# Attention and gated FFN on one core: the product with V behind the first score tile, a couple's own mark, and query couples at half rate

## The chip, the core and the metric

The kernel runs on one core of a Trainium2 chip. TensorE (PE) multiplies, VectorE (DVE) and ScalarE (ACT) read its results from PSUM banks, GpSimd (POOL) does elementwise work on SBUF, SyncE (SP) issues DMAs. The metric is the device time of one execution in microseconds; lower is better. Before the change it is 1832.74 us, the median of three runs (1832.44 to 1833.5).

## The reference

A block of a transformer with adaptive layer norm: one sequence of 2048 rows of 512, attention with 32 query heads of 16 and a single key and value head, then a gated FFN with 1792 hidden columns.

```python
mod = (_silu(c) @ w_mod).reshape(c.shape[0], 6, 1, -1)
h = _layernorm(x, axis=-1) * (1 + ca) + sa
# attention: q = h wq (32 heads of 16), k = h wk, v = h wv (one head)
scores = jnp.einsum("bhqd,bkd->bhqk", q, k) * (Dh ** -0.5)
p = _softmax(scores, axis=-1)
o = jnp.einsum("bhqk,bkd->bhqd", p, v)
x = x + ga * (o @ wo)
h = _layernorm(x, axis=-1) * (1 + cb) + sb
x = x + gb * ((_sigmoid(h @ w_gate) * (h @ w_up)) @ w_down)
```

## The kernel before, in words

**Units and half-steps.** The attention is cut into 32 units: eight blocks of 256 query rows by four groups of eight heads. A unit runs over 16 key blocks of 128 rows; one key block of one unit is a *step*, 512 in all, and a step has two *half-steps* h = 0 and 1, 1024 in all. TensorE is split for this: a matmul takes 64 rows (one *row half*) and 32 columns, so that `columns` issues four matmuls that fill one row half, and the two halves can work at once.

**What a half-step issues.** The tuple `ORDER` (line 57) gives the order:

- `a0`, `a1`: two tiles of scores for the row maxima (tile name `sa`, 128 queries by 512 keys). DVE reduces each to its maximum (`mx<-sa`). They run ahead of the rest by 84 tiles (`A0`) and so end 42 half-steps before the loop does. Three banks.
- `s0`, `s1`: two tiles of transposed scores (`st`, 128 keys by 512 query columns). ACT writes the exponential of each to `P`. Two banks, so that a half-step's `s0` needs the bank that the half-step before filled with its own `s0`.
- `c`: the product of P and V, in float32 (`craw<-P,V`), for the step two earlier (`LAG`). It adds to one bank over the whole unit. A float32 matmul runs as two passes, so the trace has eight of them.

The score tiles use row half 1 - h and the product row half h; with every half-step they change places.

**Marks.** Two row halves must not add to one bank at the same time. So after a product `hand_over` issues a matmul with one column of zeros (`craw<-nought`) whose end raises the semaphore `turn`, and `take_over` waits until `turn` has reached the latest count, `done[0]`. The product waits so before it starts. What stands behind such a wait in the program waits too, since the instructions of an engine are issued in their order.

**Couples.** At the end of a half-step stands a *piece* of other work (`piece`, `plan`). Two groups of matmuls with a bank each, for queries (`pq`), the output product (`po`), gate and up (`pgu`) or down (`pd`), make a `Couple`: 24 *blocks* or more (a block is four matmuls on each row half). In its first leg, blocks 0 to m - 1, group 0 has row half 0 and group 1 row half 1; in the second they change halves. After the first leg a mark is handed over, before the second there is a `take_over`. A new couple uses the two banks that ACT and DVE have to empty of the last one.

**The planner.** `plan` spreads a couple's blocks over half-steps: `RATE` 2.2 a half-step, at most `MOST` 3, for FFN work; for query couples before step `FIRST` `QRATE` 0.9, at most one. Ten of the sixteen query groups are left for the loop, so there are five query couples. The FFN of a pair of units' rows (512 rows) joins once they are done; the first at step 137, the last pair's after the loop, in the tail, where matmuls are 128 x 128 and row halves are not used. What of the planned couples finds no room in the loop goes there too. Weights are loaded and split into two float16 parts on the way, one job every so many steps (`WSTEPS`); the last four, which overwrite the query weights, wait for step `WLAST`.

Of the kernel before, what the change touches and what calls it, by code (L numbers as in the profile page):

```python
# [53 lines left out]
HLO = ('PDPD', 'PPPP', 'PPPP', 'PPPP')  # L54

A0 = 84
ORDER = "a0", "c", "s0", "a1", "s1"
LAG = 2


# [3 lines left out]
GAP = 2  # L64
KEPT = 2
RATE = 2.2
QRATE = 0.9
MOST = 3
SWAP = 5
WSTEPS = 110  # L70
WLAST = 112
WLATE = 2
WSTORE = 5
FIRST = 75
QLEAD = 6
W1 = 2
W2 = 3
# [9 lines left out]
def adaln_mqa_glu_kernel(  # L87
# [48 lines left out]
    pe, dve, act = Ordered(nc.tensor), Ordered(nc.vector), Ordered(nc.scalar)  # L136
# [5 lines left out]
    def columns(dst, l_, r_, start, stop):  # L142
        for c_ in range(0, P, 32):
            pe.matmul(dst[c_:c_ + 32], l_[:, c_:c_ + 32], r_, start=start, stop=stop)

    turn, done, side, open_ = nc.alloc_semaphore("turn"), [0], [0], [False]
# [4 lines left out]
    def behind(later, earlier):  # L151
        tc.add_manual_dep(later.ins, earlier.ins.name,
                          mybir.DependencyInfo(mybir.DependencyClass.Sync, mybir.DependencyReason.DATA),
                          reason="a bank that Tile doesn't follow")

    def hand_over():
        g, rs = 32 * (done[0] // 2 % 4), slice(64 * side[0], 64 * side[0] + 64)
        z = pe.matmul(raw_c["c"][g:g + 32, 0:1], nought[rs], nought[rs, 0:1], start=False, stop=False)
        if not done[0]:
            behind(z, nought_set)  # L160
        done[0] += 1
        z.then_inc(turn, 1)
        tc.add_to_no_dep_group("turn", z.ins)
        tc.no_tile_sem_insts.add(z.ins.name)

    def take_over():
        pe.wait_ge(turn, done[0])

    class Group:
        def __init__(self, stage, n, name, term, end, begin=None, w=1):  # L170
# [17 lines left out]
    class Couple:  # L188
# [3 lines left out]
        def part(self, n0, n1):  # L192
            if n0 == 0:
                for g in self.gs:
                    g.open()
            m = self.gs[0].n
            for n in range(n0, n1):
                if n == m:
                    take_over()
                for j in range(2):  # L200
                    g = self.gs[j ^ (n >= m)]
                    l_, r_, *cut = g.term(n % m, slice(64 * j, 64 * j + 64))
                    columns(cut[0](g.bank) if cut else g.bank, l_, r_, n == 0, n == 2 * m - 1)
                if n == m - 1 and open_[0]:
                    hand_over()
            if n1 == self.n:
                for k, g in enumerate(self.gs):
                    g.end(g.bank, k == 1)
# [5 lines left out]
    def t32(name, shape=(P, 512)):  # L214
        return wp.tile(list(shape), F32, tag="f32", name=name, bufs=18)
# [284 lines left out]
    def q_group(b, o):  # L500
# [5 lines left out]
        def end(pq, second):  # L506
            qdone.add((b, o))
            q2 = wp.tile([P, 2, 512], F16, tag="q2", name="q2", bufs=2)
            q32 = t32("q32")
            if second and now[0] < FIRST:  # L510
                defer(1, lambda: q_evict(b, o, q2, q32, pq))
# [10 lines left out]
    def q_evict(b, o, q2, q32, pq):  # L522
        act.activation(q32, pq, AF.Identity, scale=1.0 / (SH * SW))
        pool.tensor_scalar(q2[:, 0], q32, 1.0, 0.0, op0=ALU.mult, op1=ALU.add)
        q_low(b, o, q2, q32)
# [110 lines left out]
    def pv(i, t, j):  # L636
        c_ = raw_c["c"]
        side[0] = j
        rs = slice(64 * j, 64 * j + 64)
        if (t, j) != (0, 0):  # L640
            take_over()
        for hh in range(4):
            z = pe.matmul(c_[32 * hh:32 * hh + 32, :], V[rs, t, :], Ps[i, t, hh][rs, :],
                          start=(t == 0 and j == 0), stop=(t == NKB - 1 and j == 1))
            if (t, j, hh) == (0, 0, 0) and i > 0:
                behind(z, raw_c["out"])
        open_[0] = (t, j) != (NKB - 1, 1)
        if open_[0]:
            hand_over()
        raw_c["last"] = z  # L650
        if j == 1:
            for hh in range(4):
                del Ps[i, t, hh]
            if t == NKB - 1:
                unit_end(i)
# [82 lines left out]
    def defer(n, f_):  # L738
        waits.append((now[0] + n, f_))
# [34 lines left out]
    class Transposes:  # L774
        stage, n = "tr", 4

        def __init__(self, part):
            self.part = part
# [214 lines left out]
    def places(m, hb, rate, most, skip, part):  # L993
        ws = []
        rate, most = rate / part, most / part
        while sum(ws) * rate < m + lead[0] / part - rate / 2 or sum(ws) * most < m:
            ws.append(0.0 if len(ws) < (skip or 0) else weight(hb + len(ws), skip is not None))
        lead[0] += part * (m - rate * sum(ws))
        ends = [round(m * sum(ws[:k + 1]) / sum(ws)) for k in range(len(ws))]
        return [k - z for z, k in zip([0] + ends, ends)]  # L1000
# [23 lines left out]
    def plan(s, hb):  # L1024
# [8 lines left out]
        else:  # L1033
            q = g.stage == "q" and s < FIRST
            rate, most = (QRATE, 1) if q else (RATE, MOST)
            sizes = []
# [22 lines left out]
    for i, (b, o) in enumerate(units):  # L1059
# [10 lines left out]
        for kb in range(NKB):  # L1070
# [12 lines left out]
            for h in range(2):  # L1083
                for z in ORDER:
                    k = int(z[1:] or 0)
# [15 lines left out]
            while wdone < nw:  # L1101
                if wdone < nw - 4 and (wdone + 0.5) * WSTEPS > (s + 1) * (nw - 4):
                    break
                if wdone >= nw - 4 and s < WLAST + 3 * (wdone - nw + 4):
                    break
# [66 lines left out]
```

## Time and profile before

| what | us |
|---|---|
| median of three runs | 1832.74 |
| the profiled execution | 1831.11 |
| its span, first to last instruction | 1829.0 |
| PE busy | 1787.7 |
| DVE busy | 1455.2 |
| ACT busy | 1241.5 |
| POOL busy | 617.8 |
| granted TensorE clock, mean | 0.993 |

The first half-step begins at 107 us, the last ends at 1671; before lies the set-up (modulation, norm, keys, first queries), behind it the tail. Line 133 is the helper that records nearly every instruction of the loop, so groups are told apart by their tiles. A row of a group gives the number of instructions, the busy time, the mean of one and the engine's idle time just before them with what ended it. The matmuls' ends are modelled; their starts are measured.

### The profile page before, as it was taken

The page shows a single profiled execution, that of the slowest core. Times are in us where ns is not written, and L with a number is a line of the kernel's source. Part 1 is how long each engine was busy: PE and PEld are TensorE (multiplying, and loading weights), DVE is VectorE, ACT ScalarE, POOL GpSimd, SP SyncE. Part 2 cuts the span into 40 slices and gives each one's busy share as a digit, 9 for nine tenths or more (in the row PEclk, how much of TensorE's full clock was granted, in tenths as well). Part 3 has the DMA queues.
Part 4 walks back from the last instruction along what each step waited for, and adds up shares of the span by engine and source line. Part 5 has one row for each costly group of instructions (what it writes and reads, how often), then busy time and mean ns, then how long its engine had stood idle before and what let it go on. Part 6 is the DMA issues. An engine that isn't in the chain of part 4 may idle for free.

```text
span 1829.0 us, 88432 instructions
## 1 busy us (share of the span) xinstructions
PE 1787.7 (98%) x40059; PEld 932.0 (51%) x40059; DVE 1455.2 (80%) x2364; ACT 1241.5 (68%) x2335; POOL 617.8 (34%) x814
## 2 busy tenths in 40 slices
PE   6999999999999999999999999999999999999998
PEld 3334444444445555555555555555555555544443
DVE  7789999999998888888898888888898888811211
ACT  5458888888877777777777777777777777774100
POOL 4434444533072321222253331232353233022423
PEclk9989999999999999999999999999999999999999
DMA  7012323311111110110111110010111110011211
GB/s 251 30 52 83 94 94 94 94 48 43 37 48 37 49 37 11 37 33 12 49 48 46 40 49 15 23 49 11 35 51 57 37 49 26 22 32 48 74 54 58
DMA packets 84676, 94.08 MB, mean 51 GB/s; under 512 B 22868, under 2 KB 63820, under 8 KB 84300
## 3 DMA queue, kind: packets, MB, share of 16 engines
q1 hardware_dynamic: 84300, 88.44, 15.5%
q8 instruction: 313, 5.13, 1.1%
q14 instruction: 63, 0.52, 0.1%
HBM read 67.82 MB, written 16.24 MB: 46 GB/s over the span
## 4 chain that ended last, share of the span: by engine, by line
PE 87%; ACT 5%; DVE 3%; issue 2%; POOL 1%; DMA 1%; SPq 0%; POOLq 0%; ACTq 0%; DVEq 0%
PE craw L133 30%; PE st L133 13%; PE pgu L133 13%; PE sa L133 12%; PE pd L133 6%; PE pgu L184 5%; ACT P L133 3%; PE pd L184 3%; PE pq L133 2%; PE po L133 2%; DVE mx L133 1%; ACT th L133 1%; DMA xall<-in_A_x_dram 1%; DVE st L133 1%; POOL h2l L351 0%
## 5 line engine op out<-in xcount | busy, mean ns | idle before, releaser
L133 DVE TENSOR_REDUCE mx<-sa 128x1 f32<-128x512 f32 x2048 | 1339.3, 686 | 163.5 <-PE st L133 74.2
L133 ACT ACTIVATE P<-st 128x512 f32<-128x512 f32 x2048 | 1113.6, 597 | 386.1 <-PE st L133 294.5
L133 PE MATMUL craw<-P,V 64*32 64x512 f32 x8192 | 1070.6, 592 | 2.7 <-ACT cs L133 1.0
L133 PE MATMUL st<-qp,kp 64*32 64x512 f16 x8192 | 812.5, 384 | 0.9 <-ACT P L133 0.2
L133 PE MATMUL sa<-kp,qp 64*32 64x512 f16 (+1 forms) x7940 | 792.8, 378 | 7.8 <-DVE mx L133 7.6
L133 PEld LDWEIGHTS <-kp 64*32 64x32 f16 x8192 | 367.1, 90 | 345.2 <-issue 221.2
L133 PEld LDWEIGHTS craw<-P,V 64*32 64x32 f32 x8192 | 242.7, 106 | 106.4 <-PE craw L133 21.3
L133 PE MATMUL pgu<-h2h,gw 64*32 64x512 f16 x5120 | 258.7, 378 | 4.9 <-ACT h L133 0.8
L133 PEld LDWEIGHTS <-qp 64*32 64x32 f16 (+1 forms) x7940 | 228.6, 92 | 57.8 <-issue 37.9
L133 PEld LDWEIGHTS <-gw 64*32 64x32 f16 x7680 | 146.4, 91 | 64.9 <-issue 18.4
L871 POOL TENSOR_SCALAR th<-th 128x512 f32<-128x512 f32 x40 | 24.7, 618 | 451.2 <-ACT th L133 391.6
L133 PE MATMUL craw<-nought 64*32 64x1 f16 x1051 | 171.7, 163 | 0.0
L133 PEld LDWEIGHTS <-nought 64*32 64x32 f16 x1051 | 98.1, 93 | 137.3 <-issue 118.0
L133 PE MATMUL pgu<-h2l,gw 64*32 64x512 f16 x2560 | 158.8, 377 | 0.5 <-POOL h2l L351 0.5
L551 POOL MEMSET qp<- 32x1024 f16 x60 | 56.7, 944 | 99.2 <-PE st L133 80.8
L315 POOL TENSOR_SCALAR wst<-wst 128x512 f32<-128x512 f32 x46 | 28.4, 618 | 155.5 <-DMA wst<-in_B_w_up_dram 84.6
L184 PE MATMUL pgu<-h2h,gw 128*128 128x512 f16 x256 | 77.9, 385 | 2.3 <-DMA out_dram<-ot 2.3
L133 PE MATMUL pd<-wdl,gh 64*32 64x512 f16 x1152 | 75.4, 377 | 0.0
L133 PE MATMUL pd<-wdh,gl 64*32 64x512 f16 x1152 | 74.6, 377 | 0.0
L133 DVE COPY u<-pgu 128x512 f32<-128x512 f32 x40 | 27.4, 685 | 58.6 <-PE pgu L133 57.4
L133 PE MATMUL pd<-wdh,gh 64*32 64x512 f16 x1152 | 72.5, 378 | 1.5
L865 ACT ACTIVATE th<-pgu 128x512 f32<-128x512 f32 x16 | 9.6, 597 | 90.3 <-PE pgu L184 90.3
(159 smaller groups left out, 1410.4 us busy)
## 6 DMA issues: line engine op xcount, KB each, us to landing
gw<-wD SPq DMA_DIRECT2D x56, 512.0 KB
wD<-gw SPq DMA_DIRECT2D x14, 512.0 KB
wm<-in_w_mod_dram SPq DMA_DIRECT2D x6, 1024.0 KB
qp<-qD SPq DMA_DIRECT2D x192, 32.0 KB
qD<-q SPq DMA_DIRECT2D x16, 256.0 KB
xr<-in_A_x_dram SPq DMA_DIRECT2D x16, 256.0 KB
out_dram<-ot SPq DMA_DIRECT2D x16, 256.0 KB
raw<-cs SPq DMA_DIRECT2D x248, 16.0 KB
```

What stands on the lines that cost most here:

```text
L133: return (lambda *a, **k: keep(f_(*a, **k))) if pinned else f_
L184: pe.matmul(cut[0](self.bank) if cut else self.bank, l_, r_, start=(n == 0), stop=(n == self.n - 1))
L315: pool.tensor_scalar(w_, w_, SW, 0.0, op0=ALU.mult, op1=ALU.add)
L551: eng.memset(qp[j:j + 32], 0.0)
L865: act.activation(th, p_, AF.Tanh, scale=0.5 / (SH * SW))
L871: pool.tensor_scalar(th, th, 1.0, 1.0, op0=ALU.add, op1=ALU.mult)
```

## The change

The order of a half-step becomes a0, s0, c, a1, s1. A couple remembers the count of the mark that its own first leg handed over (`self.since`) and its second leg waits for that one instead of for the latest; where no mark was handed over, it waits for the latest as before. Query couples run at 0.45 blocks a half-step, and two numbers go with that: `FIRST` becomes 136, `WLAST` 150.

```diff
-ORDER = "a0", "c", "s0", "a1", "s1"
+ORDER = "a0", "s0", "c", "a1", "s1"
...
-QRATE = 0.9
+QRATE = 0.45
...
-WLAST = 112
+WLAST = 150
...
-FIRST = 75
+FIRST = 136
...
-    def take_over():
-        pe.wait_ge(turn, done[0])
+    def take_over(since=None):
+        pe.wait_ge(turn, done[0] if since is None else since)
...
                 if n == m:
-                    take_over()
+                    take_over(self.since)
...
-                if n == m - 1 and open_[0]:
-                    hand_over()
+                if n == m - 1:
+                    self.since = None
+                    if open_[0]:
+                        hand_over()
+                        self.since = done[0]
```

On PE, a half-step in the middle of the FFN work, before (each tile's first matmul and what it waits for; the rows left out are its other columns and the weight loads; `craw` is the product, `Activation` and `DVE` are the engines that must have emptied a bank):

```order
L133 MATMUL sa_22503<-kp_133,qp_20603 32x512 [waits DVE_49]
...
L133 MATMUL craw<-P0_22267,V_134 32x512 [waits turn]
L133 MATMUL craw<-P1_22280,V_134 32x512
...
L133 MATMUL craw<-nought 32x1
...
L133 MATMUL st_22515<-qp_18969,kp_133 32x512 [waits Activation_49]
...
L133 MATMUL sa_22521<-kp_133,qp_20603 32x512 [waits DVE_49]
...
L133 MATMUL st_22527<-qp_18969,kp_133 32x512 [waits Activation_49]
...
L133 MATMUL pgu_22086<-h2l_13023,gw_20987 32x512
```

And after, on PE, at the same place of another unit:

```order
L133 MATMUL sa_22675<-kp_133,qp_21897 32x512 [waits Activation_49]
...
L133 MATMUL st_22681<-qp_18645,kp_133 32x512 [waits Activation_49]
...
L133 MATMUL craw<-P0_22421,V_134 32x512 [waits turn]
L133 MATMUL craw<-P1_22440,V_134 32x512
...
L133 MATMUL craw<-nought 32x1
...
L133 MATMUL sa_22693<-kp_133,qp_21897 32x512 [waits DVE_49]
...
L133 MATMUL st_22699<-qp_18645,kp_133 32x512 [waits Activation_49]
```

The first `st`, with its wait for ACT, moved ahead of the product and of the product's wait for `turn`; the second `sa` and `st` stand behind the product and its mark in both.

On PE in the early part, where query couples (`pq`) fill the half-steps, before: two half-steps in a row end with blocks.

```order
L133 MATMUL st_1439<-qp_171,kp_133 32x512 [waits Activation_49]
...
L133 MATMUL pq_1329<-h1h0_384,wdl_76 32x512
...
L133 MATMUL pq_1330<-h1h0_384,wdl_76 32x512
...
L133 MATMUL craw<-P0_1285,V_134 32x512 [waits turn]
...
L133 MATMUL st_1477<-qp_171,kp_133 32x512 [waits Activation_49]
...
L133 MATMUL pq_1329<-h1h1_399,wdh_75 32x512
...
L133 MATMUL pq_1330<-h1h1_399,wdh_75 32x512
```

After, on PE, between the same two blocks of the couple:

```order
L133 MATMUL pq_1392<-h1h0_384,wdl_76 32x512
...
L133 MATMUL pq_1393<-h1h0_384,wdl_76 32x512
...
L133 MATMUL craw<-P0_1411,V_134 32x512 [waits turn]
...
L133 MATMUL st_1597<-qp_171,kp_133 32x512 [waits Activation_49]
...
L133 MATMUL craw<-P0_1411,V_134 32x512 [waits turn]
...
L133 MATMUL pq_1392<-h1h1_399,wdh_75 32x512
...
L133 MATMUL pq_1393<-h1h1_399,wdh_75 32x512
```

A half-step without blocks, with its own product, now lies between the two. The blocks of a couple and their number are the same; over the whole program 24 blocks, one gate and up couple, are no longer in the loop but stand as 24 matmuls of 128 x 128 in the tail. The wait of the second leg stands where it stood; only the count that it waits for is lower.

## The prediction

> **What bounds the kernel now.** I read the page first, then a table of stretches, then single half-steps in the timeline, then the waits of ACT and DVE.
>
> ```profile
> span 1829.0 us, 88432 instructions
> PE 1787.7 (98%) x40059; PEld 932.0 (51%) x40059; DVE 1455.2 (80%) x2364; ACT 1241.5 (68%) x2335; POOL 617.8 (34%) x814
> PE 87%; ACT 5%; DVE 3%; issue 2%; POOL 1%; DMA 1%; SPq 0%; POOLq 0%; ACTq 0%; DVEq 0%
> ```
>
> PE looks full, but eight sub-arrays of 64x32 work side by side here and "busy" only says that one of them is. So the half-step has to be taken apart. The stretches (columns: length, then busy time and instructions of PE, PEld, DVE, ACT, POOL) follow the stages: score passes with query couples, score passes almost alone, score passes with feed-forward (FFN) couples, the last half-steps without max tiles, the tail.
>
> ```profile
> 124.00:305.00 181.00, 180.46 (x4044) 83.45 (x4033) 166.66 (x269) 146.30 (x278) 74.77 (x93) 1.00 0.27 83
> 305.00:483.00 178.00, 176.76 (x3459) 74.73 (x3444) 171.75 (x281) 149.56 (x282) 68.00 (x87) 1.00 0.20 59
> 483.00:1602.00 1119.00, 1109.14 (x29500) 629.23 (x29488) 980.98 (x1560) 820.41 (x1556) 345.06 (x444) 1.00 0.12 37
> 1602.00:1671.00 69.00, 67.94 (x1540) 32.83 (x1543) 7.13 (x13) 50.30 (x95) 18.31 (x21) 1.00 0.11 31
> 1671.00:1829.00 158.00, 149.46 (x711) 67.64 (x703) 28.84 (x49) 15.34 (x29) 56.18 (x66) 0.99 0.19 63
> ```
>
> In 305:483 DVE is busy 171.75 of 178 us, 96.5%: there it is the bound. In 483:1602, 61% of the span, it is busy 980.98 of 1119 (87.7%) and ACT 73%: nothing is full. Exponentials, two to a half-step, count the half-steps (the same windows, ACT on tile st):
>
> ```profile
> 124.00:305.00 181.00, 139.66 (x258) 1.00 0.27 83
> 305.00:483.00 178.00, 145.02 (x268) 1.00 0.20 59
> 483.00:1602.00 1119.00, 768.18 (x1413) 1.00 0.12 37
> 1602.00:1671.00 69.00, 47.80 (x88) 1.00 0.11 31
> ```
>
> 1413/2 = 706.5 half-steps in 1119 us: 1.584 us each. What is lost in one shows in the timeline (start, length):
>
> ```profile
> 809.46 0.39 PE L133 MATMUL sa<-kp,qp 64*32 64x512 f16 x4
> 809.64 0.61 PE L133 MATMUL craw<-P,V 64*32 64x512 f32 x4
> 809.68 0.40 PE L133 MATMUL st<-qp,kp 64*32 64x512 f16 x4
> 809.90 0.40 PE L133 MATMUL sa<-kp,qp 64*32 64x512 f16 x4
> 809.94 0.69 DVE L133 TENSOR_REDUCE mx<-sa 128x1 f32<-128x512 f32 x1
> 810.07 0.61 PE L133 MATMUL craw<-P,V 64*32 64x512 f32 x4
> 810.17 0.40 PE L133 MATMUL st<-qp,kp 64*32 64x512 f16 x4
> 810.51 0.16 PE L133 MATMUL craw<-nought 64*32 64x1 f16 x1
> 810.87 0.69 DVE L133 TENSOR_REDUCE mx<-sa 128x1 f32<-128x512 f32 x1 [0.24 <-PE st L133]
> 810.87 0.60 ACT L133 ACTIVATE P<-st 128x512 f32<-128x512 f32 x1 [0.75 <-PE st L133]
> 811.52 0.40 PE L133 MATMUL st<-qp,kp 64*32 64x512 f16 x4
> ```
>
> The program's order here is sa, craw (the product), mark, st, sa, st. The first sa stands ahead of the product, and its maximum starts 0.48 us after it (809.46 to 809.94). The first st stands behind the product: its matmuls end at 810.08, but its exponential starts at 810.87, and so does the maximum of the second sa, though ACT had idled 0.75 us. Both start 0.19 after the product's second pass ends (810.07 + 0.61 = 810.68). So PE's completion signals come in program order even though its two row halves run past each other; the first score tile is held 0.79 us by a product it has nothing to do with.
>
> That closes a loop. The product starts at 809.64; the exponential at +1.23; 0.60 later the bank is free, and the next half-step's first st, which needs it, starts at 811.52, +1.88 (its slot, 0.22 behind its sa, was 811.15). On its row half follow second sa (+0.22), second st (+0.27), 0.22 of its own and two blocks of the couple (0.43, a block taking 0.215: rows at 838 below) and then the product of the half-step after next: 1.88 + 1.14 = 3.02 for two half-steps, 1.51 each. Without that wait a half-step with two blocks looks like this one:
>
> ```profile
> 838.62 0.61 PE L133 MATMUL craw<-P,V 64*32 64x512 f32 x4
> 838.65 0.39 PE L133 MATMUL sa<-kp,qp 64*32 64x512 f16 x4
> 838.87 0.39 PE L133 MATMUL st<-qp,kp 64*32 64x512 f16 x4
> 839.05 0.61 PE L133 MATMUL craw<-P,V 64*32 64x512 f32 x4
> 839.30 0.39 PE L133 MATMUL st<-qp,kp 64*32 64x512 f16 x4
> 839.91 0.40 PE L133 MATMUL sa<-kp,qp 64*32 64x512 f16 x3
> ```
>
> 838.65 to 839.91 is 1.26 us: four tiles of 0.215 on one half, two passes of 0.43 on the other, two blocks on both. That is PE's own need.
>
> **The change, part by part.**
>
> *Product behind the first score tile.* Nothing is added; four loads and four matmuls are issued earlier on PE. The first st is then signalled behind its sa alone: its exponential starts about 0.48 after it instead of 1.19, ends at 1.08, well ahead of the next slot 1.26 later. The loop is gone. What is next: the second st is still signalled behind the product, so its bank is free at product + 1.23 + 0.60 + 0.05 = 1.88; with 0.22 of matmul and 0.43 of blocks that makes 2.53 for two half-steps, 1.265, no more than PE's need. On PE a half-step costs 1.26, plus 0.215 x 0.06 for the mean of 2.06 blocks that the changed program's order has here, plus stalls at a couple's edges (its first leg waits for two banks that ACT and DVE empty; a first leg's mark makes the next product late): with some 0.5 us per couple, 24/2.06 = 11.7 half-steps, 0.04. Together 1.32. DVE needs 980.98/706.5 = 1.389, and at the 96.5% at which it saturates in 305:483, 1.439. So DVE becomes the bound. I take 1.455, one per cent above, for stalls that its three banks don't bridge: (1.584 - 1.455) x 706.5 = **-91 us**. Ends: 1.40 (DVE at 99%), -130; 1.526 (rival 1), -41.
>
> Queued behind the moved product on PE: mark, second sa, second st, blocks. The product now waits in line behind st, which waits for ACT. The cover is that the exponential ends before the slot; if not, rival 2.
>
> In 305:483 DVE is the bound already: 0. In 1602:1671 there are no maxima; 88/2 = 44 half-steps take 1.57, the same loop without its sa steps; ACT's 50.30 us are the floor: between 0 and -16 us, I take **-8**, the middle.
>
> *Own mark for the second leg.* Before, the second leg waits for the mark of the product just issued:
>
> ```profile
> 803.96 0.40 PE L133 MATMUL st<-qp,kp 64*32 64x512 f16 x4
> 804.18 0.16 PE L133 MATMUL craw<-nought 64*32 64x1 f16 x1
> 804.45 0.41 PE L133 MATMUL pgu<-h2h,gw 64*32 64x512 f16 x8
> ```
>
> The st would have let it start at 803.96 + 0.215 = 804.18; it starts at 804.45: 0.27 us, with all that is queued behind on PE. About 706.5/11.7 = 60 couples, 16 us at most. After, the awaited mark was already awaited by the product before it. This lies inside the 1.584 and in the 1.32, so it adds nothing to the -91 as long as DVE is the bound.
>
> *Query couples at half rate.* 124:305 holds 129 half-steps at 1.40 with DVE at 92%. With 0.41 blocks instead of 0.79 and no score wait, DVE's 166.66 us at 96.5% take 172.7: **-8** (ends 0 and -12). The couples now fill half-steps up to 290; in 305:483 a half-step takes 178/134 = 1.33, and four tiles with 0.4 blocks need 0.86 + 0.09 on PE: 0. The q stores and the pieces of their evictions on ACT and POOL are the same number, spread out; the first of these query blocks is loaded at step 133 and is made by step 27, the last couple's, made by step 145, at 357: 0. The four last splits of the down weights move 38 steps back, on POOL (31% busy) and DMA (12%): 0, and even uncovered they are used only in the second half of the down product. FFN starts 17 half-steps later, so one couple, 24 blocks, falls out of the loop into the tail, where it is 24 full matmuls:
>
> ```profile
> 1690.14 0.59 PE L184 MATMUL pgu<-h2h,gw 128*128 128x512 f16 x2
> 1690.57 0.38 PE L184 MATMUL pgu<-h2l,gw 128*128 128x512 f16 x1
> 1690.79 0.59 PE L184 MATMUL pgu<-h2h,gw 128*128 128x512 f16 x2
> ```
>
> Three in 0.65 us, 0.216 each: **+5**.
>
> Sum: -91 - 8 - 8 + 5 = -102. The profiled execution took 1831.1 us (2.1 around its span), 1.6 below the median of the runs: 1831.1 - 102 = 1729, or 1731 by the median. I say 1730.
>
> **A rule against it.** The mark at 810.51 stands ahead of the st at 809.68, the sa and the st at 810.17 in the program, and starts after all three: starts are not in program order across row halves, signals are. The Trainium skill, TensorE: Matmul & The Clock Gate, section The mechanism, says "MATMULs are pc-monotone in start AND end — strict FIFO, no reordering." For the ends the signals above agree; for the starts these rows do not. What strict order of starts would give is rival 3.
>
> **Rivals.**
>
> 1. *Half the gain.* The waits on ACT and DVE:
>
> ```profile
> ACT P L133 <- PE st L133: 237.8, 396, 1.6
> DVE mx L133 <- PE st L133: 65.4, 248, 0.5
> ```
>
> The 65.4 us of the second maximum behind the product stay, since it stays behind it. If edge stalls of a couple (1.0 us: 0.5 at the start, 0.5 at the mark) add to DVE's 1.439 and don't lie beside it, a half-step is 1.439 + 1.0/11.7 = 1.525: -42 us; with -4, -4 and +5, 1786. For it: ACT gets the couple's eviction between two exponentials. Against: three sa banks let DVE lag by about one maximum, 0.69.
>
> 2. *Slower: the product inherits ACT's wait.* The st at 811.52 is 0.37 behind its slot. If the first exponential stays late for another reason than the product, the product starts behind it, 0.59 after sa; 0.59 + 0.86 + 0.43 = 1.88 per half-step, +0.30 x 706.5 = +209 us, 2040. It decides when the exponential starts later than 1.26 - 0.60 = 0.66 after its st on the average. Against: a tile ahead of the product takes 0.48, and ACT would be 820.41/1028 = 80% busy.
>
> 3. *Nothing moves.* If matmuls started strictly in order, the product's second pass (0.43 after its first) would hold the later tiles in both orders: before 0.43 + 3 x 0.215, after 0.215 + 0.43 + 2 x 0.215, both 1.075 with the blocks on top; only the 16 us of the second legs go, less the 5 of the tail: 1820. The 1.26 at 838.65, below 1.075 + 0.43, speaks against it.
>
> **Chances.** The forecast (1700 to 1755) 0.66; rival 1 (1755 to 1810) 0.21; still faster, below 1700 (DVE at 99% throughout, 1831 - 130 - 16 - 12 + 5 = 1678) 0.03; rival 3, 0.03; rival 2, 0.06, in all its degrees; no change within 0.2% 0.01. The range reaches from 1700 into rival 1, to 1788, and holds about 0.79. Two tenths of a per cent, 3.7 us, is about what a measurement can tell here: faster 0.93, same 0.01, slower 0.06.
>
> **What would show it.** Right: in the timeline the first exponential starts about 0.5 after its st, ahead of the product's end; ACT's wait on st falls from 237.8 to below 120; DVE's share in the FFN stretch goes from 88% to 95%; the stretch has about 1.455 per half-step; the second leg's blocks follow the last st by 0.22; the tail is 5 us longer. Wrong: exponentials that start early while a half-step still takes 1.5 (PE dispatch or couple edges are the bound), or products that start 0.4 and more after their sa (rival 2).

## The result and the profile after

The changed kernel takes 1716.69 us (median, 1714.09 to 1717.44) against 1832.59 us: a ratio of 0.9364, 95% interval 0.9348 to 0.9381. That is 116 us less; 1730 had been forecast, in a range of 1700 to 1788.

The page of the changed kernel: span, busy times, the chain that ended last, and the groups of the maxima and the exponentials.

```profile
span 1715.4 us, 88057 instructions
PE 1667.8 (97%) x39888; PEld 996.6 (58%) x39888; DVE 1409.5 (82%) x2364; ACT 1290.5 (75%) x2335; POOL 616.3 (36%) x812
PE 85%; DVE 5%; ACT 3%; POOL 3%; DMA 1%; issue 1%; SPq 1%; POOLq 0%; ACTq 0%; DVEq 0%
L133 DVE TENSOR_REDUCE mx<-sa 128x1 f32<-128x512 f32 x2048 | 1293.4, 683 | 99.2 <-PE st L133 43.5
L133 ACT ACTIVATE P<-st 128x512 f32<-128x512 f32 x2048 | 1166.7, 598 | 221.3 <-PE st L133 163.9
```

Nothing in these lines says where 114 us of the span went: PE is as "busy" as before. The stretches do. Both kernels are cut at the same half-steps (12, 140, 274, 980, 1023; lines for the early stretch, the next, the FFN stretch, the loop's end, the tail), first the kernel before, then the changed one:

```profile
124.50:305.00 180.50, 179.96 (x4031) 83.20 (x4017) 166.18 (x268) 145.93 (x277) 74.77 (x93) 1.00 0.27 83
305.00:483.30 178.30, 177.06 (x3467) 74.85 (x3455) 172.05 (x281) 149.84 (x283) 68.00 (x87) 1.00 0.20 59
483.30:1602.50 1119.20, 1109.29 (x29512) 629.40 (x29514) 981.18 (x1561) 820.55 (x1556) 345.49 (x445) 1.00 0.12 37
1602.50:1670.20 67.70, 66.74 (x1519) 32.20 (x1505) 6.22 (x12) 49.08 (x94) 17.88 (x21) 1.00 0.10 31
1670.20:1829.00 158.80, 150.20 (x720) 67.97 (x714) 29.25 (x50) 16.14 (x30) 56.18 (x66) 0.99 0.19 63
```

```profile
124.80:289.00 164.20, 161.59 (x3638) 84.35 (x3630) 159.00 (x268) 147.10 (x272) 67.63 (x85) 1.00 0.27 83
289.00:460.50 171.50, 168.62 (x3812) 89.35 (x3798) 166.23 (x282) 154.27 (x285) 62.04 (x79) 1.00 0.21 62
460.50:1493.90 1033.40, 1022.00 (x29536) 678.81 (x29530) 948.58 (x1560) 860.17 (x1557) 360.18 (x463) 1.00 0.14 41
1493.90:1551.40 57.50, 56.08 (x1358) 28.91 (x1339) 6.48 (x12) 51.63 (x94) 16.58 (x18) 1.00 0.15 45
1551.40:1715.40 164.00, 154.56 (x748) 70.16 (x747) 29.52 (x50) 16.60 (x30) 54.29 (x64) 1.00 0.17 58
```

| half-steps | before | after | difference | forecast |
|---|---|---|---|---|
| 12 to 140, query couples | 180.5 | 164.2 | -16.3 | -8 |
| 140 to 274 | 178.3 | 171.5 | -6.8 | 0 |
| 274 to 980, FFN couples | 1119.2 | 1033.4 | -85.8 | -91 |
| 980 to 1023, no maxima | 67.7 | 57.5 | -10.2 | -8 |
| tail | 158.8 | 164.0 | +5.2 | +5 |
| set-up and first half-steps | 124.5 | 124.8 | +0.3 | |
| sum (span) | 1829.0 | 1715.4 | -113.6 | -102 |

Two half-steps of the FFN stretch in the timeline of the changed kernel:

```profile
791.42 0.69 PE L133 MATMUL craw<-P,V 64*32 64x512 f32 x4
791.57 0.41 PE L133 MATMUL sa<-kp,qp 64*32 64x512 f16 x4
791.79 0.41 PE L133 MATMUL st<-qp,kp 64*32 64x512 f16 x4
791.87 0.67 PE L133 MATMUL craw<-P,V 64*32 64x512 f32 x4
792.00 0.41 PE L133 MATMUL sa<-kp,qp 64*32 64x512 f16 x4
792.22 0.41 PE L133 MATMUL st<-qp,kp 64*32 64x512 f16 x4
792.31 1.74 ACT L133 ACTIVATE P<-st 128x512 f32<-128x512 f32 x3 [0.20 <-PE st L133]
792.36 0.16 PE L133 MATMUL craw<-nought 64*32 64x1 f16 x1
792.73 0.46 PE L133 MATMUL sa<-kp,qp 64*32 64x512 f16 x4
792.97 0.64 PE L133 MATMUL craw<-P,V 64*32 64x512 f32 x4
794.13 0.69 PE L133 MATMUL craw<-P,V 64*32 64x512 f32 x4
```

The exponential of the first st starts at 792.31, 0.52 after it, while the product's second pass still runs (791.87 + 0.67 = 792.54). Before, it started 0.19 after that pass had ended and 1.19 after its st. In the first of the two half-steps the tiles of a row half follow each other without a gap: 791.57, 791.79, 792.00, 792.22. Over the FFN stretch of the kernel before, 585 of 705 first st started within 0.06 us of the end of the exponential that empties their bank; now 94 do. ACT's wait for st in this stretch, 237.8 us before, is now:

```profile
ACT P L133 <- PE st L133: 131.2, 476, 4.6
```

The prediction had given "below 120" as its sign; this one is missed, though the wait is nearly halved. The second leg's blocks (pgu) now follow the last st by 0.21 and no longer wait for the product's mark at 775.33:

```profile
774.82 0.45 PE L133 MATMUL st<-qp,kp 64*32 64x512 f16 x4
775.03 0.45 PE L133 MATMUL pgu<-h2h,gw 64*32 64x512 f16 x4
775.33 0.16 PE L133 MATMUL craw<-nought 64*32 64x1 f16 x1
```

### The profile page after: what moved, and what is told of

It is laid out like the page before. It is cut to its first block, busy times and chain, and to the rows that moved or that the text cites. A ratio compares the mean times of both kernels' runs of the same rounds, so it can differ in the third digit from the quotient of the medians.

```text
span 1715.4 us, 88057 instructions
## 1 busy us (share of the span) xinstructions
PE 1667.8 (97%) x39888; PEld 996.6 (58%) x39888; DVE 1409.5 (82%) x2364; ACT 1290.5 (75%) x2335; POOL 616.3 (36%) x812
## 4 chain that ended last, share of the span: by engine, by line
PE 85%; DVE 5%; ACT 3%; POOL 3%; DMA 1%; issue 1%; SPq 1%; POOLq 0%; ACTq 0%; DVEq 0%
PE craw L133 23%; PE pgu L133 15%; PE sa L133 14%; PE st L133 13%; PE pd L133 6%; PE pgu L184 5%; DVE mx L133 3%; PE pd L184 3%; PE po L133 2%; PE pq L133 2%; ACT P L133 2%; SPq L133 1%; DMA lc<-lD 1%; POOL h2l L354 1%; DMA xall<-in_A_x_dram 1%
## 5 line engine op out<-in xcount | busy, mean ns | idle before, releaser
L133 DVE TENSOR_REDUCE mx<-sa 128x1 f32<-128x512 f32 x2048 | 1293.4, 683 | 99.2 <-PE st L133 43.5
L133 ACT ACTIVATE P<-st 128x512 f32<-128x512 f32 x2048 | 1166.7, 598 | 221.3 <-PE st L133 163.9
L133 PE MATMUL craw<-P,V 64*32 64x512 f32 x8192 | 1096.2, 601 | 1.2 <-PE craw L133 0.2
L133 PE MATMUL sa<-kp,qp 64*32 64x512 f16 (+1 forms) x7940 | 837.0, 379 | 10.9 <-DVE mx L133 10.3
L133 PE MATMUL st<-qp,kp 64*32 64x512 f16 x8192 | 838.6, 380 | 7.9 <-ACT P L133 6.2
L133 PEld LDWEIGHTS <-kp 64*32 64x32 f16 x8192 | 336.4, 91 | 227.9 <-issue 105.7
L133 PEld LDWEIGHTS <-qp 64*32 64x32 f16 (+1 forms) x7940 | 286.0, 92 | 132.6 <-issue 55.1
L133 PEld LDWEIGHTS <-gw 64*32 64x32 f16 x7488 | 171.6, 92 | 69.1 <-issue 29.4
L133 PEld LDWEIGHTS craw<-P,V 64*32 64x32 f32 x8192 | 184.7, 105 | 26.9 <-ACT cs L133 4.6
L704 POOL TENSOR_TENSOR raw<-raw 128x256 f32<-128x256 f32 x31 | 22.7, 732 | 139.1 <-DMA raw<-lD 131.6
```

The source lines that it names most:

```text
L133: return (lambda *a, **k: keep(f_(*a, **k))) if pinned else f_
L704: keep(pool.tensor_tensor(raw[:, :QU], raw[:, :QU], raw[:, QU:], op=ALU.mult))
```

## The experiments

The theory: PE's completion signals come in program order; the product held back the first score tile's; with it out of the way the loop is gone, and DVE is the next bound. The rivals: that the gain comes from the mark or the query rate; that something else than DVE bounds it now. The trials that halve an engine's work and the one with the product ahead of all tiles are single executions. The set-up with the first 12 half-steps took 118 to 128 us over the traces, and 121 to 128 where the maxima were whole, so a total can be off by some us and the stretches decide.

### The three edits apart

Order alone:

```diff
-ORDER = "a0", "c", "s0", "a1", "s1"
+ORDER = "a0", "s0", "c", "a1", "s1"
```

> The kernel before with the new order of a half-step alone (product behind the first score tile); marks and query rates as before. If the held completion signal was the loop (the prediction's first part), nearly all of the gain is here: about -75 us in the FFN stretch, -15 in the two stretches before it, -8 at the end of the loop, 1735 us (1722 to 1750). If the gain came mostly from the second leg's wait or from the query rate, under 40 us are here: above 1793.

Measured: 1724.51 us, ratio 0.9409 (0.9395 to 0.9423): 108 us of the 116. The FFN stretch took 1040.8 us, 78 less; the two before it 13.7 and 9.0 less. The rival falls.

```profile
462.20:1503.00 1040.80, 1029.47 (x29513) 648.73 (x29508) 956.34 (x1560) 864.62 (x1557) 346.13 (x445) 1.00 0.13 40
```

Own mark alone (`take_over(self.since)` and what sets it):

> The kernel before with the second leg's own mark alone. By the prediction's price (0.27 us for some 60 couples) at most 16 us: 1817 to 1830, nearer the lower end if the wait lies on the loop, nearer the upper if the score tile's wait takes up what it frees. If the second leg's half-steps owe all of their surplus over plain ones (1.96 against 1.51 us) to this wait, 25 us or more: below 1808.

Measured: 1828.84 us, ratio 0.9983 (0.9974 to 0.9993), 3 us. By the starts of the first sa in the trace, half-steps with a second leg and two blocks fell from 1.98 to 1.72 us, so the 0.26 was there, some 12 us in 48 of them. But the FFN stretch got only 4.5 us shorter:

```profile
483.50:1598.20 1114.70, 1107.44 (x29503) 632.10 (x29498) 978.36 (x1560) 820.85 (x1557) 345.47 (x445) 1.00 0.13 37
```

The 404 plain half-steps with two blocks went from 1.526 to 1.539 on the mean and the 122 with three from 1.698 to 1.720, 8 us together. That is what a loop through the score tile would take back; it was not tried apart.

Query rate alone:

```diff
-QRATE = 0.9
+QRATE = 0.45
...
-WLAST = 112
+WLAST = 150
...
-FIRST = 75
+FIRST = 136
```

> The kernel before with the query couples at half rate alone (and the two numbers that go with it). In the loop of the score wait a block costs 0.215/2 us per half-step: 0.79 to 0.41 blocks saves 0.04 x 128 = 5 us early, costs 0.03 x 134 = 4 in the next stretch unless DVE hides it, 17 half-steps of FFN work less are worth -4, the couple in the tail +5: 1825 to 1836, no gain that matters. If spreading is what frees the early stretch, 10 us or more: below 1822.

Measured: 1848.51 us, ratio 1.0089 (1.0073 to 1.0106): slower by 16 us, outside both expectations. Its stretches from half-step 140 on:

```profile
303.80:489.70 185.90, 184.72 (x3805) 82.89 (x3790) 173.09 (x281) 150.65 (x285) 61.70 (x80) 1.00 0.18 55
489.70:1613.90 1124.20, 1108.83 (x29544) 628.39 (x29545) 981.95 (x1560) 819.03 (x1557) 359.70 (x463) 1.00 0.13 38
1679.60:1844.00 164.40, 155.29 (x744) 70.24 (x738) 29.53 (x50) 16.39 (x30) 54.30 (x64) 0.98 0.17 58
```

Against before, +7.6, +5.0 and +5.6; the early stretch gave back 2.8 and the loop's end 2.0, and the set-up was 1.6 longer. Nothing hid the blocks in 140 to 274 (4 us had been the price, 7.6 came), and the FFN stretch did not gain from starting its FFN work 17 half-steps later. By the trace it did not have less work: 1470 blocks stand in it against 1466 before, and the couple that fell out is missing in the loop's end (74 blocks against 94). Why the stretch lost 5 was not tried apart.

Order and own mark, with the query rate of before:

> The changed kernel with the query couples' rate of before: new order and own mark, query rate 0.9. The order alone gave 1724.5 and all three 1716.7. If the own mark is what brings the last 8 us, this is 1710 to 1718. If the query rate brings them, it is at 1721 to 1726.

Measured: 1707.19 us, ratio 0.9317 (0.9301 to 0.9333). This is faster than the changed kernel, whose interval begins at 0.9348. So the mark is worth 17 us once the loop is gone (1724.5 to 1707.2; the intervals allow 11 to 22), some five times what it is worth with it, and the half query rate costs some 9 us (the intervals allow 3 to 15). The traced execution is the longest of the four, and its trace shows a smaller part: 12.6 us less than the order alone, all in the FFN stretch, and 5.3 less than the changed kernel. Of the latter, FFN and tail hold the difference (1033.4 and 164.0 in the changed kernel), while its set-up was 3.2 longer:

```profile
462.60:1490.70 1028.10, 1020.51 (x29508) 674.56 (x29500) 947.07 (x1560) 859.63 (x1557) 346.03 (x445) 1.00 0.14 40
1549.60:1710.10 160.50, 150.92 (x732) 68.59 (x723) 29.53 (x50) 16.32 (x30) 56.18 (x66) 0.98 0.19 63
```

### Signals in program order

The product moved the other way, ahead of all four tiles, in the kernel before:

```diff
-ORDER = "a0", "c", "s0", "a1", "s1"
+ORDER = "c", "a0", "s0", "a1", "s1"
```

> The kernel before with the product moved the other way, ahead of all four tiles: c, a0, s0, a1, s1. If signals come in program order, the first maximum is now held too: it starts 0.1 to 0.2 after the product's second pass ends, where it started 0.05 to 0.1 after its own sa ended. The loop through the first exponential is the same, so the time is 1825 to 1870. If each tile were signalled by itself, the first maximum would stay at 0.1 after its sa and the product's place would not matter: 1725 to 1835 with the early maxima.

Measured: 1863.83 us. The timeline:

```profile
900.22 0.40 PE L133 MATMUL sa<-kp,qp 64*32 64x512 f16 x4
900.40 1.04 PE L133 MATMUL craw<-P,V 64*32 64x512 f32 x8
900.86 0.40 PE L133 MATMUL st<-qp,kp 64*32 64x512 f16 x4
901.57 1.29 DVE L133 TENSOR_REDUCE mx<-sa 128x1 f32<-128x512 f32 x2 [0.20 <-PE sa L133]
901.63 1.08 ACT L133 ACTIVATE P<-st 128x512 f32<-128x512 f32 x2 [0.34 <-PE sa L133]
```

The sa starts 0.18 ahead of the product and ends at 900.62, but stands behind it in the program: its maximum starts at 901.57, 0.13 after the product's end (900.40 + 1.04). Over the loop the median of that delay is 0.91 us, where it was 0.13 before. DVE was busy with earlier maxima until 901.38, so the maximum alone could mislead. The trace also has the moments at which semaphores rise: the counter that PE raises for every tile does not rise between 900.24 and 901.55, right behind the product's mark at 901.49. In the rows of the kernel before at 809.46 it rises at 809.91 for the first sa and then, for st, sa and st, at 810.79, 810.85 and 810.91, right behind the mark at 810.73. So the signals themselves are late, and not only a wait for a count: they come in program order, on whichever row half, and the mark stands in that line with the product.

One tile further back instead, in the changed kernel (a0, s0, a1, c, s1):

> The changed kernel with the product one tile further back: a0, s0, a1, c, s1. By the signals in program order the second maximum is then released with its own tile too, and DVE never waits for the product. If that is what DVE still lacks, the FFN stretch gains 10 to 25 us: 1690 to 1707. If the product is then issued late (it stands behind the second sa, which waits for a bank that DVE frees) its start moves 0.2 us and more behind the first sa and the time rises: 1720 to 1780.

Measured: 1729.80 us, ratio 0.944 (0.9423 to 0.9456), slower than the changed kernel by 13 us. The second maximum is indeed released with its tile, but DVE's wait for sa in the FFN stretch is now 84.3 us, where the waits for sa and st together had been 54.2 (19.2 and 35.0):

```profile
DVE mx L133 <- PE sa L133: 84.3, 232, 2.8
462.30:1504.50 1042.20, 1030.16 (x29540) 706.39 (x29532) 940.10 (x1560) 853.34 (x1558) 360.13 (x463) 1.00 0.14 41
```

An earlier maximum brought nothing, and the product starts 0.03 us later on the mean (0.10 after the first sa against 0.07), which is small but falls 706 times in a stretch that took 9 us more. That speaks against DVE as the bound.

### What bounds the loop now

Maxima over half a tile, in the changed kernel and in the one before:

```diff
-        dve.tensor_reduce(mxs[i][:, 4 * j + r, qt, kc:kc + 1], sa, axis=AX.X, op=ALU.max)
+        dve.tensor_reduce(mxs[i][:, 4 * j + r, qt, kc:kc + 1], sa[:, :256], axis=AX.X, op=ALU.max)
...
-        act.activation(p_[:, j], s_, AF.Exp, scale=0.25)
+        act.activation(p_[:, j], s_, AF.Exp, scale=0.02)
```

> The changed kernel with each maximum taken over 256 of 512 columns (the other half of the keys is left out of the maximum, the exponential's scale is cut to 0.02 so that it stays finite). If DVE is what bounds the FFN stretch now, as the prediction says, its half-step falls from 1.46 to PE's need with stalls, 1.33 to 1.38, and the two stretches before it from 1.28 to below 1.2: 1600 to 1650 us. If PE with its marks and the couples' edges is the bound there, under 30 us of the FFN stretch go: 1675 to 1705.

> The kernel before with each maximum taken over 256 of a tile's 512 columns, which takes about half of DVE's time away (the maximum over the other half of the keys is left out, and the exponential's scale is cut to 0.02 so that it stays finite; ACT's and PE's instructions are the same). If DVE bounds 305:483 but not the FFN stretch (the prediction's reading), the score loop stays: FFN from 1.58 to no less than 1.53, 1785 to 1815 in all. If DVE bounds the FFN stretch too, its half-step falls to the 1.3 of PE's need: below 1700.

Measured: 1703.40 us after, 1820.95 before; 13 and 12 us less. First the two stretches of the changed kernel (half-steps 140 to 274, FFN), then those of the kernel before:

```profile
284.00:454.60 170.60, 168.12 (x3806) 85.81 (x3798) 105.31 (x281) 154.03 (x285) 62.11 (x79) 1.00 0.21 63
454.60:1480.00 1025.40, 1014.29 (x29540) 673.22 (x29531) 641.64 (x1559) 859.65 (x1558) 360.28 (x463) 1.00 0.14 42
```

```profile
298.10:476.30 178.20, 176.96 (x3459) 74.49 (x3444) 104.39 (x281) 149.81 (x283) 67.38 (x86) 1.00 0.20 59
476.30:1592.80 1116.50, 1107.71 (x29515) 628.81 (x29515) 640.62 (x1560) 820.36 (x1556) 345.71 (x445) 1.00 0.13 37
```

DVE falls from 97% to 62% of the second stretch and from 92% to 63% of the FFN stretch of the changed kernel, and they shorten by 0.9 and 8 us. In the kernel before, the stretch in which DVE had been 96.5% busy keeps its length to 0.1 us. Of the 13 and 12 us in all, 4 and 7 lie in the set-up. DVE is not the bound, and was not where it looked full.

The product over half its columns, in the changed kernel:

```diff
-        act.activation(p_[:, j], s_, AF.Exp, scale=0.25)
+        act.activation(p_[:, j], s_, AF.Exp, scale=0.02)
...
+            wide = 512 if t == 0 else 256
-            z = pe.matmul(c_[32 * hh:32 * hh + 32, :], V[rs, t, :], Ps[i, t, hh][rs, :],
+            z = pe.matmul(c_[32 * hh:32 * hh + 32, :wide], V[rs, t, :], Ps[i, t, hh][rs, :wide],
```

> The changed kernel with the product taken over 256 of 512 columns, but for a unit's first key block (half of the output's columns leave out the other key blocks; the exponential's scale is cut to 0.02 so that all stays finite). A row half carries in two half-steps four tiles of 0.215, two passes of 0.43 and four blocks of 0.215, 2.58 us. If this is what bounds the FFN stretch of the changed kernel, half the product takes 0.43 off 2.58, 0.215 per half-step: from 1.464 to 1.25 to 1.33, where ACT's and DVE's 1.2 to 1.3 come next, 90 us and more: 1590 to 1630 in all. If latencies at the couples' and units' edges or the signals behind the product are the bound, 30 us or less go: above 1685.

Measured: 1615.45 us, 101 less than the changed kernel. Half-steps 140 to 274, then the FFN stretch:

```profile
280.60:445.20 164.60, 160.00 (x3809) 77.83 (x3797) 163.78 (x282) 157.87 (x285) 61.99 (x79) 1.00 0.22 66
445.20:1396.80 951.60, 925.78 (x29531) 563.83 (x29534) 914.91 (x1560) 831.98 (x1557) 359.81 (x463) 0.99 0.15 45
```

951.6/706 = 1.348 per half-step, from 1.464: 0.116 of the 0.215 that the row halves were relieved of, a little outside the expected 1.25 to 1.33. The median of plain half-steps with two blocks fell from 1.35 to 1.17, nearly the whole 0.215. A shorter product also signals sooner, so this alone does not separate occupancy from signals; but releasing the second maximum without shortening the product had gained nothing. And in the changed kernel the first sa starts within 0.05 us of the moment at which its row half comes free (a pass counted as 0.43 and a block as 0.215) in 85% of the half-steps of this stretch, where it was 55% before. So time on the row halves is the main bound of the FFN stretch. Much of the rest stands at the edges of couples and units: there a half-step with a second leg takes 1.70, one without a block, 53 of them, 1.33. What takes over at 1.35 is open.

Exponentials over half a tile:

```diff
-        act.activation(p_[:, j], s_, AF.Exp, scale=0.25)
+        act.activation(p_[:, j, :256], s_[:, :256], AF.Exp, scale=0.25)
...
-            z = pe.matmul(c_[32 * hh:32 * hh + 32, :], V[rs, t, :], Ps[i, t, hh][rs, :],
+            z = pe.matmul(c_[32 * hh:32 * hh + 32, :].rearrange("p (r q) -> p r q", r=2), V[rs, t, :],
+                          Ps[i, t, hh][rs, :256].unsqueeze(1).to_broadcast([64, 2, 256]),
```

> The changed kernel with each exponential taken over 256 of a tile's 512 columns; the product reads that half twice, so that PE's instructions are the same (half of the attention output is therefore a copy of the other). ACT's time is about halved. With half the maxima the stretch of half-steps 140 to 274 stayed at 170.6 us of 171.5, though DVE had been busy 97% of it. If ACT, busy 90% there, is its bound, it falls from 1.28 per half-step to 1.15 to 1.2, by 10 to 17 us; if the chain of product, mark, next product is (0.86 + 0.16 and the signals), it stays above 1.25. The FFN stretch, bound by PE's row halves, should lose less than 25 us: 1675 to 1710 in all; if ACT bounds it too, more than 60 go: below 1650.

Measured: 1683.48 us, 33 less. Half-steps 140 to 274 took 164.8 us (1.23 each), between the two expectations; the FFN stretch lost 16.5 us, as little as expected. The trace shows where such a sum can lie. In the changed kernel 94 first and 221 second st of the FFN stretch still start within 0.06 us of the exponential that empties their bank, and the st start later than 0.22 behind their sa by 24 us in sum; with half the exponentials it is 13, 25 and 8 us. So the loop through the second score tile, which is still signalled behind the product, is not quite gone.

```profile
280.40:445.20 164.80, 163.41 (x3812) 84.72 (x3805) 163.31 (x282) 105.74 (x284) 62.16 (x79) 1.00 0.22 66
445.20:1462.10 1016.90, 1005.94 (x29529) 702.93 (x29535) 943.33 (x1560) 595.67 (x1556) 360.28 (x463) 0.99 0.14 42
```

### The first leg's mark

In the changed kernel, no mark after a first leg and one empty piece between the legs:

```diff
-                    self.since = None
-                    if open_[0]:
-                        hand_over()
-                        self.since = done[0]
+                    self.since = done[0] + 1
...
+                if leg and not q:
+                    sizes.append(0)
...
-RATE = 2.2
+RATE = 2.35
```

> The changed kernel without the first leg's mark: one piece without blocks is left between the legs, and the second leg waits for the mark of the product that stands between them, which the next product has awaited already; the FFN rate is 2.35 so that the loop holds the same number of blocks. In the changed kernel the product behind a first leg's mark starts 0.3 us late (0.31 after its sa, against 0.0 in plain half-steps) and its half-step takes 1.66 against 1.36. If that mark is a stall that nothing hides, 49 x 0.3 = 15 us go: 1695 to 1706. If DVE's pace hides it, the time stays within 4 us of 1716.7; if the denser pieces (more with three blocks) cost more than the mark, it rises by up to 10.

Measured: 1711.50 us, ratio 0.9338 (0.9321 to 0.9356). That is 5 us below the changed kernel, with intervals that overlap. The FFN stretch took 1027.2 us, 6 less, the tail 168.2, 4 more. But the stretch also holds 24 blocks less (1446 against 1470), which stand behind it; at 0.215 each that is an estimated 5 us of the 6:

```profile
455.60:1482.80 1027.20, 1015.56 (x29301) 660.69 (x29297) 952.17 (x1560) 857.73 (x1558) 360.31 (x463) 1.00 0.14 41
1541.70:1709.90 168.20, 158.96 (x773) 71.99 (x755) 30.19 (x51) 16.93 (x31) 57.99 (x68) 0.97 0.19 63
```

The same with the query rate of before:

> New order, no first leg's mark (one piece without blocks between the legs, FFN rate 2.35), query rate of before. If the leg's mark costs 5 us and the slow query rate nothing or a little, 1705 to 1712. If the changed kernel without the mark gained only by chance of the planner's placing, 1713 to 1722.

Measured: 1713.96 us, ratio 0.9343 (0.9324 to 0.9361), no better than with the slow query rate, and behind order and own mark alone. Its FFN stretch and tail:

```profile
461.40:1487.40 1026.00, 1015.11 (x29345) 661.12 (x29348) 953.73 (x1560) 856.12 (x1555) 346.61 (x446) 1.00 0.14 40
1545.50:1712.30 166.80, 157.43 (x748) 70.78 (x747) 29.47 (x50) 16.50 (x30) 54.32 (x64) 0.98 0.17 57
```

Against order and own mark alone the FFN stretch is 2.1 shorter, with 13 blocks less, and the tail 6.3 longer: the planner found no room for one more gate and up couple, which stands in the tail as 24 full matmuls. The pieces are denser too: 199 half-steps of the FFN stretch have three blocks, 122 with the mark, at 1.59 us each. So neither run prices the mark by itself: inconclusive, and no improvement.

## Why the prediction was right, and where not

**The held signal: right.** The order alone brought 108 us; the exponential starts 0.52 after its st, 0.48 had been said; with the product ahead of all tiles the first maximum is held too. The loop of 1.51 us was the bound of the FFN stretch: five of six first st there started as soon as their bank was empty.

**What comes next: wrong, though the number was close.** The step that failed is "DVE needs 980.98/706.5 = 1.389, and at the 96.5% at which it saturates in 305:483, 1.439. So DVE becomes the bound." With half the maxima that stretch did not get shorter, so 96.5% was no saturation, and neither is DVE the bound of the changed kernel: its share there is 92%, not the 95% that was given as a sign. In its place stand PE's row halves. "PE's own need" was read as 1.26 from one half-step; but the halves change places, and a first sa may start while the other half still works. Counted over two half-steps a row half carries four tiles, two passes and four blocks, 2.58 us; in the rows above the product on the same half comes back after 2.71 (791.42 to 794.13). So 1.29 is the need, and by the starts in the trace the median plain half-step with two blocks takes 1.35, the one with three 1.56. With edges the forecast had PE at 1.32, and 1.464 was measured. That 1.455 came so close is luck: two errors met, a floor of DVE that does not hold, and one of PE set too low.

**Where DVE was called the bound, "0" was wrong.** Half-steps 140 to 274 got 6.8 us shorter, the early stretch 16.3 instead of 8. There too the loop through the score tile had cost; the order alone gave 9.0 and 13.7. Between 140 and 274 two limits now lie close together. PE's row halves need only 0.95 of the 1.28 a half-step, and half the maxima take 0.9 us off the 171.5; half the exponentials take 6.7, half the product 6.9. In the changed kernel 127 of the 134 second st start within 0.06 us of the exponential that empties their bank; with half the exponentials 33 do, with half the product 50. In both of these DVE is busy 99% of the stretch, at 1.23 a half-step. So a chain through product and exponentials holds 1.28, and DVE stands right behind it: to that extent DVE's floor is real, at 1.23 and not at the 1.33 where it was read. Which link of the chain decides was not tried apart.

**The own mark: the size depends on the loop.** "0.27 us" a couple was measured as 0.26. "Adds nothing to the -91 as long as DVE is the bound" failed with its condition: PE is the main bound, and the mark brings 17 us on top of the order, 3 alone.

**The query rate: wrong in sign.** Costed at -8 early and +5 in the tail, it costs some 9 us in the changed kernel and 16 alone. The tail's 5 was right (5.2). That the early stretch still gained more than the 8 forecast is luck, since the gain came from the order: with the order and the query rate of before the two stretches take 165.4 + 169.2 us, in the changed kernel 164.2 + 171.5.

**Rivals.** Half the gain did not come: the couples' edges and DVE's waits lie on a stretch that DVE does not bound. The product did not inherit ACT's wait: the first st starts 0.22 after its sa in half of all FFN half-steps and later than 0.29 in one of twenty. Strict order of starts is out: the mark at 792.36 starts after the sa and the st at 792.00 and 792.22, which stand behind it in the program.

Order and own mark with the query rate of before, 1707 us, is the best kernel of this study.

## What to carry to other kernels

Where one engine works on several things at once but reports them in program order, put the short piece that others wait for ahead of the long one, and look in the timeline for consumers that start just after an unrelated instruction's end. A unit that is busy 97% of a stretch is not thereby its bound: halve its work and see whether the stretch gets shorter. Edits that are shipped together should be timed apart: here one gave nearly all, one was worth some five times as much behind it, and one cost time.

## What was not expected of the hardware

- DVE's busy time overstates its need. A lone maximum of a 128x512 tile takes 0.69 us, but those that start before the one ahead has ended start 0.60 apart (the median of 1377 in the changed kernel). The stretch that showed 97% in 171.5 us did the same maxima in 164.6 with half the product.
- A completion signal is held by an earlier matmul even on the other row half: the exponential of the first st before started 0.79 us after the st's end, and with the product first the counter rose 0.93 us after the end of the sa (900.62 to 901.55). Signals that were held come 0.06 us apart.
